# 64-column tiles and three early weight conversions in a gated linear attention with two MLPs

## The chip, the cores and the metric

The kernel runs on one core of a Trainium2 chip. The metric is the device time of one execution in microseconds. Five engines take part: PE (matmuls, with its weight loads shown apart as PEld), DVE (VectorE), ACT (ScalarE), POOL (GpSimd) and SP, which issues most DMAs. Each takes its own instructions in program order and waits on semaphores for the others.

## The reference

A linear attention with a decay for each key channel runs over 4 batches, 8 heads, 768 steps and 48 channels. Its output, laid out as 3072 tokens of 384, goes through two gated MLPs of 1536 hidden channels, the second after an RMS norm. The MLP weights come in double precision.

```python
def _attn_ref(q, k, v, alpha):
    for t in range(S):
        state = alpha[:, :, t, :, None] * state + np.einsum('bhd,bhe->bhde', k[:, :, t], v[:, :, t])
        y[:, :, t] = np.einsum('bhd,bhde->bhe', q[:, :, t], state)

def _moe_ref(x, w_gate, w_val, w_out):
    g = x @ w_gate
    silu = g * (1.0 / (1.0 + np.exp(-g)))
    val = x @ w_val
    return (silu * val @ w_out).astype(np.float32)

def _moe2_ref(x, w_gate, w_val, w_out, rms_g):
    rms = np.sqrt(np.mean(x * x, axis=-1, keepdims=True) + 1e-06)
    xn = x / rms * rms_g
    ...  # then as _moe_ref
```

## The kernel before

**Attention.** The sequence is cut into 24 chunks of 128 steps (`n`), with the four head pairs `p` side by side and the two heads of a pair on partitions 0 to 63 and 64 to 127. Inside a chunk the terms between steps are built in levels `b` = 1, 2, 4, ... 64 (`LEVELS`): at level b the second half of each block of 2b steps attends to the first half. `products` and `merge` on DVE keep the decays and scale q and k for each level, `copy_qk` on ACT packs the operands of a level, `scores` (L301) makes the score tiles on PE, `masks` (L314, DVE) and `copies_32`, `copies_64` (ACT) bring them to SBUF as `P`, and `outputs` (L357) multiplies them with v into the tile `Y` in PSUM. The first six chunks use all seven levels; the others use five and do the terms inside blocks of four steps directly on DVE (`direct_ops`), bringing them to PE over DRAM (`ydd`, `yn`). `own_terms` puts these terms into `Y` by three transposes (L342) and, from chunk 4 on, adds the terms of the carried state (L346). `kv` (L371) multiplies k^T with v for the new state; `state` (DVE) adds it up.

**Tiles of the array.** Outputs and state terms are made in 12 blocks of 32 columns of weights (`blocks32`), a block for each third of a pair's 96 columns; k^T v in 16 tiles of 32 columns; scores in tiles of 64 rows by 32 columns. All of this is fp32, which PE does in two records per matmul: 12 blocks of a level are 24 records.

**MLP.** `mlp_points` goes through the blocks of chunks (`BLOCKS`: 2, 2, 4, 4, 4, 4, 4 chunks for the first MLP, six of 4 for the second) and, in each, through the 12 slices `f` of the hidden channels: gate matmuls (tile g), silu on ACT (L704), value matmuls (tile v, both L697), multiplication s = s*v on DVE (L707), and, one slice late, the output matmuls (`out_piece`, L738). g and v have one PSUM buffer each, so the gate of the next slice waits for silu and its value for the multiplication. The first two blocks (`PLAIN`) use fp32 weights and 256 columns; later ones use weights split into two fp32r parts.

**Conversion.** `conv(0)` turns the double-precision weights of slice f into fp32 in three steps: ACT takes the absolute value (L169); ACT takes the exponent byte (L175) and DVE clamps (L176); DVE puts the bits together (L185, L191) and the load of slice f + 3 is issued on POOL's queue. The first three loads are issued on SP's queue when the generator starts.

**Order.** Everything is emitted in one hand-written order. `lead` does chunks 0 and 1 together, before any MLP work. `slot(s)` emits step T of chunk n, with T = s - 12(n - 1), twelve slots for each chunk: merges at T = 1 to 6, scores at 6 and 9, transposes of k at 12, own terms and part of the outputs at 14, k^T v and the rest at 16. Slots below `START` come before the MLP; the others are spread over its points, three for each f, so that a block of four chunks takes along 48 slots. While the first block runs, each point also takes 1.1 conversion steps (`CONV1`), and a gate matmul whose slice isn't converted forces the missing steps ahead of it:

```python
while first and self.ready32 <= f:
    next(self.cv[0])
```

In `lead` one conversion is done: three single steps at T == 5, after the outputs of levels 3 and 4, and after `split_x`. SP's queue loads in this order: q and k of chunks 0 and 1, the mask, the operands of the direct terms, the identity, all 14 tiles of v for the levels (`vl`), q and k of chunk 2, then nine pieces of raw weights.

Of the kernel before, what the change touches and what calls it, by code (L numbers as in the profile page):

```python
# [24 lines left out]
NP = H // 2  # L25
# [19 lines left out]
START = NS + 2  # L45
# [11 lines left out]
class Kernel:  # L57
# [94 lines left out]
    def conv(self, layer):  # L152
# [10 lines left out]
        R = {f: self.raw(layer, f) for f in range(ahead)}  # L163
# [111 lines left out]
    def scores(self, n, ls):  # L275
# [3 lines left out]
        for l in ls:  # L279
# [4 lines left out]
            if (n, part) not in self.sct:  # L284
                pool, tag = (self.ps, f"o{part}") if n == 1 else (self.ps2, "sc")
                self.sct[n, part] = pool.tile([128, 4, NP, 32], F32, tag=tag, name="sb" if part else "sa")
# [16 lines left out]

    def masks(self, n, ls):
        for l in ls:
# [4 lines left out]
            if n == 1:  # L310
                self.P[n, l] = p = self.second["pt"][:, l - NX] if l >= NX else self.second["ptx"][:, l]
            else:
                self.P[n, l] = p = self.pt[:, l - NX] if l >= NX else self.ptx[l]
            self.nc.vector.tensor_tensor(  # L314
# [5 lines left out]
    def copies_32(self, n):  # L320
        p32 = self.P[n, NL - 2] = self.second["pt32"] if n == 1 else self.pt32
        sc = self.sc.pop((n, NL - 2))
        for o in range(0, 128, 32):
            g = slice(o % 64, o % 64 + 32)
            self.nc.scalar.activation(out=p32[o:o + 32, :, g], in_=sc[o:o + 32], func=AF.Copy)
# [5 lines left out]
    def blocks32(self):  # L331

        for cb in range(3 * NP):
            yield cb // 3, slice(32 * (cb % 3), 32 * (cb % 3) + 32), cb // 4, 32 * (cb % 4)

    def own_terms(self, n):
# [7 lines left out]
        if n >= B:  # L344
            for p, e, kt, o in self.blocks32():
                nc.tensor.matmul(out=Y[o:o + 32, kt], lhsT=self.Sd[:, p].rearrange("d h e -> d (h e)")[:, e],  # L346
                                 rhs=self.q(n)[:, 0, p], start=False, stop=False, skip_group_check=True)

    def outputs(self, n, ls):
        for l in ls:  # L350
            b = LEVELS[l]
            if b < CDS[n]:
                continue
            pt = self.P.pop((n, l))
            for p, e, kt, o in self.blocks32():
                ov = self.Yt[n][o:o + 32, kt].rearrange("e (j u i) -> e j u i", u=2, i=b)[:, :, 1]
                self.nc.tensor.matmul(out=ov, lhsT=self.vl(n, l)[:, p, e], rhs=pt[:, p],  # L357
                                      start=False, stop=False, skip_group_check=True)
# [3 lines left out]
    def kv(self, n):  # L362

        nc = self.nc
        kv = self.ps.tile([128, NP, D], F32, tag="v", name="kv") if n == 1 else self.ps2.tile(
            [128, NP, D], F32, tag="sc", name="kv")
# [159 lines left out]
    def transposes(self, n):  # L526
        kp = self.kp[n] = self.ps.tile([128, NP, 128], F32, tag="g", name="kp") if n == 1 else self.ps2.tile(
# [13 lines left out]
    def lead(self):  # L541
# [6 lines left out]
        direct = {}  # L548
        for T in range(1, NL):
            for n in two:  # L550
                self.scores(n, [T - 1])
# [13 lines left out]
            if T == 5:  # L565
                next(self.cv[0])
        for n in two:
            self.scores(n, [NL - 1])
# [17 lines left out]
        next(self.cv[0])  # L586
        for n in two:
            self.kv(n)
        for n in two:
# [6 lines left out]
        self.load_qk(3)  # L596

# [157 lines left out]
    def run(self):  # L755
# [59 lines left out]
        for i in range(NS, START):  # L815
            self.slot(i)
# [100 lines left out]
```

## Time and profile before

| | us |
|---|---|
| median of 3 runs | 1140.61 |
| lowest, highest | 1139.85, 1142.17 |
| the profiled execution | 1139.1 |
| its span, first to last instruction | 1137.3 |

The profile gives, for one execution, each engine's busy time, groups of instructions by source line, the chain of waits that ended last, and every instruction in order of time. Weight loads overlap matmuls and stand apart. A matmul's recorded duration is the time through the whole array, so for small tiles many overlap and the spacing of starts tells the rate. "issue" as the releaser of a wait means that the engine waited for nothing that the profile shows.

### The profile page before, as it was taken

The page shows a single profiled execution, that of the slowest core. Times are in us where ns is not written, and L with a number is a line of the kernel's source. Part 1 is how long each engine was busy: PE and PEld are TensorE (multiplying, and loading weights), DVE is VectorE, ACT ScalarE, POOL GpSimd, SP SyncE. Part 2 cuts the span into 40 slices and gives each one's busy share as a digit, 9 for nine tenths or more (in the row PEclk, how much of TensorE's full clock was granted, in tenths as well). Part 3 has the DMA queues.
Part 4 walks back from the last instruction along what each step waited for, and adds up shares of the span by engine and source line. Part 5 has one row for each costly group of instructions (what it writes and reads, how often), then busy time and mean ns, then how long its engine had stood idle before and what let it go on. Part 6 is the DMA issues. An engine that isn't in the chain of part 4 may idle for free.

```text
span 1137.3 us, 29157 instructions
## 1 busy us (share of the span) xinstructions
PE 1086.9 (96%) x12756; PEld 891.1 (78%) x12756; DVE 652.7 (57%) x1350; ACT 413.8 (36%) x737; POOL 39.5 (3%) x69
## 2 busy tenths in 40 slices
PE   3688898999999999999999999999999999999997
PEld 3567787788888888887888888888888888888886
DVE  6588798777676766766746877723322323233221
ACT  3556544433343343334334444422231222322212
POOL 0121000000000000000000000000000000000000
PEclk9899999999999999999999999999999999999999
DMA  9677344543443454345315343110000000100000
GB/s 335 196 224 223 100 134 137 150 135 105 135 142 104 113 156 134 105 128 148 104 58 192 114 143 122 42 56 1 29 28 1 29 29 1 56 1 1 29 1 28
DMA packets 55665, 112.72 MB, mean 99 GB/s; under 512 B 7185, under 2 KB 38929, under 8 KB 55537
## 3 DMA queue, kind: packets, MB, share of 16 engines
q1 hardware_dynamic: 51072, 93.15, 27.2%
q0 software_dynamic: 4464, 17.70, 4.7%
q8 instruction: 100, 1.64, 0.6%
q14 instruction: 29, 0.23, 0.1%
HBM read 97.85 MB, written 12.98 MB: 97 GB/s over the span
## 4 chain that ended last, share of the span: by engine, by line
PE 82%; DMA 1%; issue 1%; DVE 1%; ACT 0%; POOLq 0%; DVEq 0%; ACTq 0%
PE g L697 25%; PE v L697 24%; PE o L738 24%; PE y L357 3%; PE sb L301 2%; PE y L346 1%; PE sa L301 1%; PE kv L371 1%; PE y L342 1%; DMA yn<-ydd 1%; PE rb L636 0%; PE kp L530 0%; PE ss L617 0%; DMA ydd<-yd 0%; DMA out<-ev 0%
## 5 line engine op out<-in xcount | busy, mean ns | idle before, releaser
L707 DVE TENSOR_TENSOR s<-s,v 128x512 f32<-128x512 f32 (+1 forms) x156 | 100.8, 646 | 371.2 <-PE v L697 370.0
L697 PE MATMUL g<-xhi,w 128*128 128x512 f32 x792 | 270.7, 396 | 0.0
L697 PE MATMUL v<-xhi,w 128*128 128x512 f32 x792 | 269.7, 395 | 0.0
L738 PE MATMUL o<-hh,w 128*128 128x512 f32 x792 | 201.8, 390 | 0.0
L704 ACT ACTIVATE s<-g 128x512 f32<-128x512 f32 (+1 forms) x156 | 88.1, 565 | 289.4 <-PE g L697 286.7
L713 ACT ACTIVATE hh<-s 128x512 fp32r<-128x512 f32 x132 | 83.5, 633 | 271.1 <-DVE s L707 271.0
L697 PEld LDWEIGHTS g<-xhi,w 128*128 128x128 f32 x792 | 148.6, 188 | 33.0
L697 PEld LDWEIGHTS v<-xhi,w 128*128 128x128 f32 x792 | 148.8, 188 | 32.4
L738 PEld LDWEIGHTS o<-hh,w 128*128 128x128 f32 x792 | 148.8, 188 | 31.7
L697 PE MATMUL v<-xlo,w 128*128 128x512 f32 x396 | 154.7, 391 | 0.0
L697 PE MATMUL g<-xlo,w 128*128 128x512 f32 x396 | 154.5, 390 | 0.0
L719 DVE TENSOR_TENSOR hl<-s,hh 128x512 fp32r<-128x512 f32 x132 | 91.0, 689 | 41.4 <-ACT hh L713 36.8
L738 PE MATMUL o<-hl,w 128*128 128x512 f32 x396 | 114.4, 397 | 0.2 <-DVE hl L719 0.2
L697 PEld LDWEIGHTS g<-xlo,w 128*128 128x128 f32 x396 | 74.5, 188 | 14.9
L697 PEld LDWEIGHTS v<-xlo,w 128*128 128x128 f32 x396 | 74.4, 188 | 14.7
L738 PEld LDWEIGHTS o<-hl,w 128*128 128x128 f32 x396 | 72.7, 188 | 16.6 <-DVE hl L719 0.6
L273 ACT ACTIVATE kc<-qk 128x512 f32<-128x512 f32 x69 | 43.7, 633 | 67.1 <-DVE qk L248 64.9
L248 DVE TENSOR_TENSOR qk<-qk,bpb 128x512 f32<-128x512 f32 x96 | 65.6, 683 | 4.3 <-ACT kc L273 2.2
L697 PE MATMUL g<-x,x 128*128 128x256 f32 x144 | 38.3, 403 | 16.2 <-DVE x L191 16.1
L357 PE MATMUL y<-pt,vl 128*32 128x64 f32 x2760 | 49.6, 222 | 2.3 <-issue 2.3
L357 PEld LDWEIGHTS y<-pt,vl 128*32 128x32 f32 x2760 | 44.0, 112 | 5.0 <-issue 4.3
L697 PEld LDWEIGHTS g<-x,x 128*128 128x128 f32 x144 | 26.8, 197 | 22.3 <-issue 16.9
(129 smaller groups left out, 1098.5 us busy)
## 6 DMA issues: line engine op xcount, KB each, us to landing
vl<-vl SPq DMA_DIRECT2D x115, 192.0 KB, 4.8
qk<-qka SPq DMA_DIRECT2D x42, 288.0 KB, 5.0
room<-w SPq DMA_DIRECT2D x27, 384.0 KB, 4.5
room<-w POOLq DMA_DIRECT2D x27, 384.0 KB, 4.3
dir<-dirx SPq DMA_DIRECT2D x54, 192.0 KB, 3.2
wraw<-w SPq DMA_DIRECT2D x18, 384.0 KB, 3.8
x2in<-x2d SPq DMA_DIRECT2D x6, 768.0 KB, 4.3
out<-ev SPq DMA_DIRECT2D x18, 256.0 KB, 2.0
```

The source lines that it names most:

```text
L248: self.nc.vector.tensor_tensor(out=v, in0=v, in1=sub(t, o, [(1, 2), (2, nb), (0, b)]), op=ALU.mult)
L273: self.nc.scalar.activation(out=sub(t, 0, [(NP * 64, 2), (b, NP * 64 // b), (1, b)]), in_=v, func=AF.Copy)
L301: nc.tensor.matmul(out=sc[o:o + 32, p], lhsT=kc[d, p, gs], rhs=qc[d, p, gs if b < 64 else slice(0, 64)], start=True, stop=True, skip_group ...
L342: nc.tensor.matmul(out=Y[:, k], lhsT=yn[:, 128 * k:128 * k + 128], rhs=self.ident, is_transpose=True, start=(k == 0), stop=False, skip_gro ...
L346: nc.tensor.matmul(out=Y[o:o + 32, kt], lhsT=self.Sd[:, p].rearrange("d h e -> d (h e)")[:, e], rhs=self.q(n)[:, 0, p], start=False, stop= ...
L357: self.nc.tensor.matmul(out=ov, lhsT=self.vl(n, l)[:, p, e], rhs=pt[:, p], start=False, stop=False, skip_group_check=True)
L697: nc.tensor.matmul(out=ps[:, :N], lhsT=a, rhs=x, start=(q == 0), stop=(q == len(ops) - 1))
L704: nc.scalar.activation(out=s[:, :N], in_=g[:, :N], func=AF.Silu)
L707: nc.vector.tensor_tensor(out=s[:, :N], in0=s[:, :N], in1=v[:, :N], op=ALU.mult)
L713: nc.scalar.activation(out=hh[:, :N], in_=s[:, :N], func=AF.Copy)
L719: nc.vector.tensor_tensor(out=hl[:, :N], in0=s[:, :N], in1=hh[:, :N], op=ALU.subtract)
L738: nc.tensor.matmul(out=O[gj][i][:, :N], lhsT=a[:, 128 * i:128 * i + 128], rhs=x[:, :N], start=(f == 0 and q == 0), stop=(f == NF - 1 and q ...
```

## The change

- `outputs`, the state terms in `own_terms` and `kv` use tiles of 64 columns where a head's columns allow: `columns(64)` gives four blocks of 64 columns, `columns(32)` the four of 32 that are left. In each call all blocks of 64 come first, then all of 32. `kv` uses 8 tiles of 64 columns.
- In chunks 0 and 1 `scores_two` makes 64 by 64 score tiles in place of pairs of 64 by 32, with whole masks; two levels share a PSUM tile, and the tiles lie in other PSUM buffers.
- The lead takes nine conversion steps instead of three, so slices 0, 1 and 2 stand ahead of the MLP in program order. One more slot (T = 2 of chunk 2) lies ahead of it too (`START`), each of the three slots behind a conversion step.
- The raw weights of the first slices are loaded earlier in SP's queue: slice 0 after eight of the 14 `vl` tiles, slice 1 after the other six, slice 2 after q and k of chunk 2.

```diff
-START = NS + 2
+START = NS + 3
...
-        R = {f: self.raw(layer, f) for f in range(ahead)}
+        R = {f: self.raw(layer, f) for f in range(ahead)} if layer else self.R0
...
+    def scores_two(self, l):
+        b = LEVELS[l]
+        for n in range(2):
+            if l % 2 == 0:
+                self.sct[n] = (self.ps2.tile([128, 2, NP, 64], F32, tag="sc", name="st") if l in (0, NL - 1) else
+                               self.ps.tile([128, 2, NP, 64], F32, tag=("g", "v", "o0", "o1")[l - 2 + n], name="st"))
+            t = self.sc[n, l] = self.sct[n][:, l % 2]
...
+            for p in range(NP):
+                for h in range(2):
+                    d = slice(64 * h, 64 * h + 64)
+                    self.nc.tensor.matmul(out=t[d, p], lhsT=k[d, p], rhs=q[d, p], start=True, stop=True,
+                                          skip_group_check=True)
...
-    def blocks32(self):
-
-        for cb in range(3 * NP):
-            yield cb // 3, slice(32 * (cb % 3), 32 * (cb % 3) + 32), cb // 4, 32 * (cb % 4)
+    def columns(self, w):
+        for p in (0, 2, 1, 3):
+            for e in ((0, 64) if p % 2 == 0 else (32, 0)):
+                if (w == 64) == (e == 32 or e == 0 and p % 2 == 0):
+                    o = 96 * p + e
+                    yield p, slice(e, e + w), o // 128, slice(o % 128, o % 128 + w)
...
     def outputs(self, n, ls):
+        ls = [l for l in ls if LEVELS[l] >= CDS[n]]
+        for w in (64, 32):
+            for l in ls:
+                for p, e, kt, o in self.columns(w):
+                    ov = self.Yt[n][o, kt].rearrange("e (j u i) -> e j u i", u=2, i=LEVELS[l])[:, :, 1]
+                    self.nc.tensor.matmul(out=ov, lhsT=self.vl(n, l)[:, p, e], rhs=self.P[n, l][:, p],
+                                          start=False, stop=False, skip_group_check=True)
...
-                for o in (64 * h, 64 * h + 32):
-                    nc.tensor.matmul(out=kv[o:o + 32, p], lhsT=kt[:, p, o:o + 32], rhs=vn[:, p, h],
-                                     start=True, stop=True, skip_group_check=True)
+                o = slice(64 * h, 64 * h + 64)
+                nc.tensor.matmul(out=kv[o, p], lhsT=kt[:, p, o], rhs=vn[:, p, h],
+                                 start=True, stop=True, skip_group_check=True)
...
         for n in two:
             self.outputs(n, range(3, 5))
-        next(self.cv[0])
+        step()
         for n in two:
             self.merge(n, LEVELS[-1])
             self.products(n, LEVELS[-1])
             self.transposes(n)
+        step()
...
-        next(self.cv[0])
         for n in two:
             self.kv(n)
+        step()
+        step()
         for n in two:
             self.state(n)
...
         self.load_qk(3)
+        step()
+        for i in range(NS, START):
+            step()
+            self.slot(i)
...
         for n in range(2):
-            for l in range(NL):
+            for l in range(4):
                 self.load_vl(n, l)
+        self.R0 = {0: self.raw(0, 0)}
+        for n in range(2):
+            for l in range(4, NL):
+                self.load_vl(n, l)
+        self.R0[1] = self.raw(0, 1)
         self.load_qk(2)
+        self.R0[2] = self.raw(0, 2)
```

## Rows read from the trace of the kernel before

**Rows 1.** The page: busy time of PE (part 1), the chain that ended last (part 4).
```profile
PE 1086.9 (96%) x12756; PEld 891.1 (78%) x12756; DVE 652.7 (57%) x1350; ACT 413.8 (36%) x737; POOL 39.5 (3%) x69
...
PE 82%; DMA 1%; issue 1%; DVE 1%; ACT 0%; POOLq 0%; DVEq 0%; ACTq 0%
```
**Rows 2.** Stretches: length, busy us (instructions) by engine, granted clock, DMA share, GB/s.
```profile
0.00:41.70 41.70, 20.36 (x862) 17.08 (x862) 23.12 (x53) 16.52 (x30) 2.49 (x9) 1.00 0.84 293
...
51.00:123.40 72.40, 62.38 (x1189) 51.76 (x1190) 58.76 (x97) 41.28 (x60) 13.57 (x24) 0.96 0.64 204
123.40:207.00 83.60, 77.43 (x1750) 64.00 (x1749) 70.39 (x160) 39.83 (x80) 2.60 (x4) 0.98 0.50 137
307.00:357.00 50.00, 50.00 (x850) 40.35 (x850) 35.23 (x87) 19.95 (x41) 2.60 (x4) 1.00 0.46 134
```
**Rows 3.** PE in time: start, us, line, tiles, weights, shape, count; chunk 9's attention.
```profile
245.27 0.49 PE L342 MATMUL y<-ident,yn 128*128 128x128 f32 x3
245.69 0.86 PE L346 MATMUL y<-qk,Sd 128*32 128x128 f32 x24
246.36 0.85 PE L357 MATMUL y<-pt,vl 128*32 128x64 f32 x48
247.15 0.50 PE L697 MATMUL g<-xhi,w 128*128 128x512 f32 x1
247.48 0.40 PE L697 MATMUL g<-xlo,w 128*128 128x512 f32 x1
...
249.43 0.55 PE L371 MATMUL kv<-vn,kt 128*32 128x48 f32 x32
249.80 1.19 PE L357 MATMUL y<-pt,vl 128*32 128x64 f32 x72
```
**Rows 4.** PE in time, the lead and the first MLP block; idle time before in brackets.
```profile
20.48 0.66 PE L301 MATMUL sb<-kc 64*32 64x32 f32 x32
...
28.98 0.34 PE L301 MATMUL sb<-qk 64*32 64x32 f32 x9 [3.10 <-issue]
...
34.36 0.77 PE L357 MATMUL y<-pt,vl 128*32 128x64 f32 x41 [1.37 <-issue]
...
41.52 0.28 PE L371 MATMUL kv<-more 128*32 128x48 f32 x3 [1.95 <-issue]
41.72 1.56 PE L697 MATMUL g<-x,x 128*128 128x256 f32 x6
43.12 1.46 PE L697 MATMUL v<-x,x 128*128 128x256 f32 x6
50.98 2.90 PE L697 MATMUL g<-x,x 128*128 128x256 f32 x6 [6.40 <-DVE x L191]
...
123.36 1.46 PE L697 MATMUL g<-x,x 128*128 128x256 f32 x6
```
**Rows 5.** The page, part 3: the queue that brings instructions.
```profile
q8 instruction: 100, 1.64, 0.6%
```
**Rows 6.** DVE in time, the first MLP block.
```profile
46.15 0.76 DVE L176 TENSOR_SCALAR x<-x 128x1152 f32<-128x1152 f32 x1 [0.32 <-ACT x L169]
46.82 0.41 DVE L707 TENSOR_TENSOR s<-s,v 128x256 f32<-128x256 f32 x1
...
48.09 1.36 DVE L185 SCALAR_TENSOR_TENSOR x<-x,room 128x1152 int32<-128x1152 int32 x1
49.48 1.36 DVE L191 SCALAR_TENSOR_TENSOR x<-room,x 128x1152 int32<-128x1152 int32 x1
...
55.41 0.42 DVE L707 TENSOR_TENSOR s<-s,v 128x256 f32<-128x256 f32 x1 [1.37 <-PE v L697]
...
104.29 0.42 DVE L707 TENSOR_TENSOR s<-s,v 128x256 f32<-128x256 f32 x1
```
**Rows 7.** The page, part 5: the group whose waits for conversions are added up.
```profile
L697 PE MATMUL g<-x,x 128*128 128x256 f32 x144 | 38.3, 403 | 16.2 <-DVE x L191 16.1
```
**Rows 8.** PE in time, the second MLP block: two of its waits.
```profile
176.55 0.62 PE L342 MATMUL y<-ident,yn 128*128 128x128 f32 x3 [2.40 <-DMA yn<-ydd]
...
206.53 0.38 PE L301 MATMUL sa<-kc 64*32 64x32 f32 x21 [1.30 <-issue]
```

More of the change, by code (lines that the diff above doesn't have):

```diff
@@ L284, in scores @@
             if (n, part) not in self.sct:
-                pool, tag = (self.ps, f"o{part}") if n == 1 else (self.ps2, "sc")
-                self.sct[n, part] = pool.tile([128, 4, NP, 32], F32, tag=tag, name="sb" if part else "sa")
+                self.sct[n, part] = self.ps2.tile([128, 4, NP, 32], F32, tag="sc", name="sb" if part else "sa")
             t = self.sct[n, part]
@@ L313, in masks @@
                 self.P[n, l] = p = self.pt[:, l - NX] if l >= NX else self.ptx[l]
+            if n < 2:
+                self.nc.vector.tensor_tensor(out=p, in0=self.sc.pop((n, l)),
+                                             in1=self.mask[:, l:l + 1].to_broadcast([128, NP, 64]), op=ALU.mult)
+                continue
             self.nc.vector.tensor_tensor(
@@ L324, in copies_32 @@
             g = slice(o % 64, o % 64 + 32)
-            self.nc.scalar.activation(out=p32[o:o + 32, :, g], in_=sc[o:o + 32], func=AF.Copy)
+            self.nc.scalar.activation(out=p32[o:o + 32, :, g], in_=sc[o:o + 32, :, g] if n < 2 else sc[o:o + 32], func=AF.Copy)
     def copies_64(self, n):
@@ L344, in own_terms @@
         if n >= B:
-            for p, e, kt, o in self.blocks32():
-                nc.tensor.matmul(out=Y[o:o + 32, kt], lhsT=self.Sd[:, p].rearrange("d h e -> d (h e)")[:, e],
-                                 rhs=self.q(n)[:, 0, p], start=False, stop=False, skip_group_check=True)
+            for w in (64, 32):
+                for p, e, kt, o in self.columns(w):
+                    nc.tensor.matmul(out=Y[o, kt], lhsT=self.Sd[:, p].rearrange("d h e -> d (h e)")[:, e],
+                                     rhs=self.q(n)[:, 0, p], start=False, stop=False, skip_group_check=True)
     def outputs(self, n, ls):
-        for l in ls:
[L351 to L358, printed above, removed]
+        ls = [l for l in ls if LEVELS[l] >= CDS[n]]
+        for w in (64, 32):
+            for l in ls:
+                for p, e, kt, o in self.columns(w):
+                    ov = self.Yt[n][o, kt].rearrange("e (j u i) -> e j u i", u=2, i=LEVELS[l])[:, :, 1]
+                    self.nc.tensor.matmul(out=ov, lhsT=self.vl(n, l)[:, p, e], rhs=self.P[n, l][:, p],
+                                          start=False, stop=False, skip_group_check=True)
+        for l in ls:
+            del self.P[n, l]
         if n == CDS.index(4) - 1 and NL - 1 in ls:
@@ L364, in kv @@
         nc = self.nc
-        kv = self.ps.tile([128, NP, D], F32, tag="v", name="kv") if n == 1 else self.ps2.tile(
+        kv = self.ps.tile([128, NP, D], F32, tag=f"o{n}", name="kv") if n < 2 else self.ps2.tile(
             [128, NP, D], F32, tag="sc", name="kv")
@@ L526, in transposes @@
     def transposes(self, n):
-        kp = self.kp[n] = self.ps.tile([128, NP, 128], F32, tag="g", name="kp") if n == 1 else self.ps2.tile(
+        kp = self.kp[n] = self.ps.tile([128, NP, 128], F32, tag="gv"[n], name="kp") if n < 2 else self.ps2.tile(
             [128, NP, 128], F32, tag="sc", name="kp")
@@ L547, in lead @@
             self.products(n, 1)
-        direct = {}
+        step = lambda: next(self.cv[0])
         for T in range(1, NL):
-            for n in two:
-                self.scores(n, [T - 1])
+            self.scores_two(T - 1)
             for n in two:
@@ L565, in lead @@
             if T == 5:
-                next(self.cv[0])
-        for n in two:
-            self.scores(n, [NL - 1])
+                step()
+        self.scores_two(NL - 1)
         for n in two:
@@ L596, in lead @@
         self.load_qk(3)
+        step()
+        for i in range(NS, START):
+            step()
+            self.slot(i)
     def norm_steps(self, j):
@@ L814, in run @@
         self.lead()
-        for i in range(NS, START):
-            self.slot(i)
         cur = None
```

5 lines of the change are left out of this document (4 added, 1 removed).

## The prediction

> **What bounds the kernel now.** I read the page first: TensorE (PE) is busy for nearly the whole span, and the chain that ended last runs over it for 82% [rows 1]. Busy time alone doesn't say what a stretch waits for, so the second view is the table of stretches [rows 2]. It shows three regimes. In the lead (0 to 41.7 us) PE works half the time. From 51.0 to 123.4, the first MLP block, PE is idle for 10.0 us while VectorE (DVE) works 58.8 of 72.4. From about 207 on PE is full: 50.00 of 50.00 in the sample stretch, with DVE at 35. So every PE nanosecond counts after 207, DVE's order counts before 123, and between them both are near full.
>
> The third view is PE in order of time through one chunk's attention in the full regime [rows 3]. The three transposes of L342 start at 245.27 and end 0.49 later; one of 128 columns takes 0.107 (half of the 0.214 below), so the third starts at 245.48. The first state pass (L346, 32 columns of weights) starts at 245.69, not at 245.59: **a drain of about 0.10 us where the tile shape changes** from 128 to 32 columns. From L346 to L357, both 128 by 32, there is none: 24 passes fill 0.67 us, and 24 x 0.107 / 4 is 0.64, so four passes run side by side and the rest, 0.03, is the first weight load. L357 confirms it: 72 passes in 1.19 us, of which a single one takes 0.22, are 13.7 ns each. A pass over 256 columns costs (1.46 - 0.39) / 5 = 0.214 [rows 4], 64 columns 0.0535, and that is 3.9 times 13.7 ns. Going back to 128 columns costs another 0.10 beyond the drain, because the first g takes 0.33 to the second start where the next take 0.23.
>
> The fourth view is PE in the lead [rows 4]. There are three stalls that nothing releases ("issue"): 3.10, 1.37 and 1.95 us. The instruction queue moved 1.64 MB in 100 transfers [rows 5]; over the 25512 PE records that is 64 bytes each, 256 instructions a transfer. The stalls fall where small tiles use instructions up fast while the DMA carries 293 GB/s [rows 2]: I read them as PE waiting for its own code.
>
> The last view is DVE in the first block [rows 6]: conversion, s multiply and slot work go through one queue in program order. PE waits there for L191, the conversion's end, nine times and 16.1 us in all [rows 7].
>
> **The change, part by part. 1. Tiles of 64 columns.** A level has 12 blocks of 32 now, 24 passes, four at a time: 6 steps of 0.056 us (four of the 13.7 ns above). After it are 4 blocks of 64 (8 passes, two at a time: 4 steps) and 4 of 32 (8 passes, four at a time: 2 steps). Again 6 steps. State terms come out as 6 steps of 0.109 both ways. k^T v goes from 32 passes in 8 steps to 16 passes in 8 steps, if the 64-column weight load (half of 0.107 = 0.054) keeps up with a 48-column step (0.043): 0 to 0.10 dearer, I take 0.05. **The work streams for as long as before; a third of the instructions go, but in the full regime no stall of PE for them is visible** (PE 50.00 of 50.00 [rows 2]), so that is worth nothing there.
>
> What is added are changes of tile shape. At T = 14 the order becomes 128, 64 and 32 (state), 64 and 32 (outputs), 128: three more changes. At T = 16: 128, 64 (k^T v, outputs), 32, 128: one more. No row shows 64 to 32. The nearest rows are the change to 32 columns, 0.10 and 0.03 for the load, so 0.12 to 0.13, and the change back to 128, 0.21. I take 0.12 into 32 and 0.15 into 64 (its load is twice as long); the ends are nothing (a 64-column tile as two neighbours of 32) and 0.21. Per chunk: T = 14 gives 2 x 0.12 + 0.15 + 0.03 (the first load is longer) = 0.42; T = 16 gives 0.12 + 0.03 + 0.05 = 0.20. Behind 207 us lie chunks 8 to 23, the last four without k^T v: 12 x 0.62 + 4 x 0.57 = 9.7. Chunks 6 and 7 add 1.2. Chunks 4 and 5 add nothing: PE waits 2.40 at 176.55 for yn to come over DRAM [rows 8], which absorbs them. Chunks 2 and 3 lie in DVE's stretch. **Sum +10.9, with ends of +2 and +17.**
>
> The Trainium skill, "TensorEngine Tiling (Array Packing)", Key Properties, says that changing the tiling mode, not just the tile, drains the engine. By that rule 64 to 32 drains as 128 to 32 does in the rows, the sum stands, and the zero end falls; it speaks against this change.
>
> **2. The lead.** Its PE instructions fall from 1724 (862 records of each kind [rows 2]) to 988: 224 passes of scores, 224 of outputs, 32 of k^T v and 14 transposes, each with a load. I let the three stalls go, -6.4. Against that, 64 by 64 score tiles run two at a time, where four 64 by 32 ran: the passes here take twice their later time ((0.66 - 0.24) / 31 = 13.5 ns a pass), which is the lower of the two clock levels, 1.2 of 2.4 GHz, though the column of the granted clock has 1.00 for this stretch; so a level of both chunks goes from 0.9 to 1.7, twice on the path: +1.6. With changes of shape, +0.2. The MLP's first matmul moves from 41.72 to about 37.
>
> There the gain stops. Behind it DVE has, in program order, the rest of f = 1 (L185 and L191, 1.36 each), all of f = 2 (0.76 + 1.36 + 1.36 [rows 6]), the states and slots 12 to 15: some 11 us from about 38.5, when ScalarE (ACT) has delivered its part. The first s multiply and the g of f = 1 stand behind that, as ACT's silu stands behind the copies of the same slots. s lands near 50 (46.82 now), g of f = 1 near 49.6 (50.98 now), the second s near 55.5 (55.41 now). POOL's loads of the weights for f = 3 and on follow each conversion and come earlier; SP's order of loads puts the first weights ahead of six vl tiles, which are wanted only at about 30 us. Both I cost at nothing; without that cover, one weight load of 1.18 MB at 293 GB/s is 4 us.
>
> **3. Conversions two ahead.** The rate stays 1.1 steps a point, so DVE's order per f is as now until f = 8 instead of 10. From the second to the ninth s takes 48.9 us (55.41 to 104.29); of the DVE idle in it, about 3.4 us come from PE being late, the rest from ACT. So the ninth lands at 55.5 + 45.5 = 101. After that no conversion is left and PE sets the pace: the 19.1 us to the next block's g at 123.36 [rows 4] shrink by the 2.4 that PE waits for L191 in them, to 16.7. The second block begins at 117.7: **-5.7**, with ends of -1 (DVE keeps its idle time) and -13 (PE sets the pace throughout). DVE's idle time at the end of the first block is what remains.
>
> **4. Later fetch stalls.** 1.30 at 206.53 [rows 8] and 0.24 before it lie in scores that stay as they are, but fewer instructions precede them: 0 to -1.5, I take -0.8.
>
> Sum on the profiled execution: 1139.1 + 10.9 - 5.7 - 0.8 = 1143.5, +4.4. That execution lies 1.5 below the median of 1140.6, so the median to expect is **1145.0**.
>
> **The rivals.** (a) *64 to 32 drains nothing*, since both are made of 32-column strips. Part 1 falls to +2, the sum is -4.5: 1136. For it: within one shape neighbouring strips run freely. Against: the drain from 128 to 32 is there although both use all 128 rows. (b) *PE sets the pace in the first block*: with conversions ahead, the 10.0 us of PE idle from 51.0 to 123.4 and the stretch at the lower clock (0.96 granted) go, and block two begins near 111, -12.5: 10.9 - 12.5 - 0.8 = -2.4, 1138. It decides where DVE's work per f (6.1) is below PE's (5.3 of matmuls and attention); the rows say above. (c) *Weight loads of the halves don't run side by side*: then 20 steps of outputs per chunk take 0.107 instead of 0.056 and k^T v 0.5 more, 1.5 us per chunk, 18 chunks, +27: 1172. Against: four 32-column loads already fit a 0.056 step, though 0.027 each. (d) *The lead's stalls stay*, because they are no matter of PE's code or because the DMA queues hold the next block back as before: part 2 loses its 6.4, DVE's chain begins some 3 us later, and the time is 1148. Against: 256 instructions of mostly 64-column work last twice as long. The Trainium skill, "Runtime: NRT & Kernel Launch", Instruction fetch mechanics, calls the cost of crossing a 16 KiB instruction block mostly hidden, which would make the stalls something else; the 3.10 and 1.95 us at such blocks do not agree with it. (e) *It doesn't do what it says*: f = 2 is converted only in program order when the MLP begins; that is in the forecast, which has DVE finish it some 10 us into the MLP.
>
> **How the numbers follow.** Forecast (1141 to 1151): 0.55. (a) 0.17, (b) 0.13, (c) 0.07, (d) 0.05, anything else 0.03. About 0.2%, 2.3 us, is what a measurement can tell from no change, so "same" is 1138.3 to 1142.9. Slower: 0.43 of the forecast, (c) and (d), together 0.55. Same: 0.11 of the forecast, 0.06 of (a), 0.06 of (b), 0.01: 0.24. Faster: 0.01, 0.11, 0.07, 0.02: 0.21. The range leaves out (c) and the far part of (a): 1135 to 1153.
>
> **What would show it.** PE in order of time past 207: one chunk's attention longer by 0.6 us, with about 0.1 between the 64- and the 32-column outputs; without that gap (a) is right. The lead: no issue stall over 1 us, the first g near 37, then a hole to about 50; if block two begins before 114, (b) has it. Steps of outputs at 0.107 mean (c). I'd be wrong altogether if attention past 207 got shorter: then instructions, not columns, set its pace.

## The result, and the profile after

| | before | after |
|---|---|---|
| median, runs side by side, us | 1141.39 (4 runs) | 1151.89 (4 runs) |
| lowest, highest | 1139.85, 1143.09 | 1149.75, 1152.57 |
| the profiled execution | 1139.1 | 1152.57 |
| its span | 1137.3 | 1150.8 |

The ratio is 1.0088, with a 95% interval of 1.0068 to 1.0109: slower, by 10.5 us in the medians. The two profiled spans lie 13.5 us apart: the profiled execution of before (1139.1) is shorter than all four of these runs, and that of after is the longest of its four. So some 3 us of the account below belong to these two executions. The forecast of 1145.0 had the sign and was 6.9 us short; as a difference it had 4.4 for 10.5. The median lies above the 1141 to 1151 that the forecast's own case covered, and inside the range of 1135 to 1153. For tiles64_only below, the median is that of three of its four runs: the fourth took 1379.08 us at a granted clock of 0.753.

The page of the kernel after: busy time of PE (part 1) and the queue that brings instructions (part 3).

```profile
PE 1105.8 (96%) x10996; PEld 899.0 (78%) x10996; DVE 653.0 (57%) x1350; ACT 412.8 (36%) x737; POOL 39.2 (3%) x69
...
q8 instruction: 86, 1.41, 0.5%
```

PE has 1760 records fewer than in [rows 1] and is busy 18.9 us longer. That is the first reading of this case: PE's busy time follows neither the instructions nor, as it turns out, the streamed columns alone.

The table of stretches after, cut where [rows 2] is cut: length, busy us (instructions) of PE, PEld, DVE, ACT, POOL, granted clock, DMA share, GB/s. The last line is the whole first block, from the first gate matmul of the MLP to that of block two.

```profile
0.00:37.10 37.10, 23.28 (x494) 20.09 (x494) 22.75 (x52) 16.75 (x31) 2.50 (x9) 0.86 0.89 317
49.90:121.80 71.90, 64.49 (x1045) 52.78 (x1046) 56.81 (x97) 37.81 (x58) 10.00 (x18) 0.93 0.57 186
307.00:357.00 50.00, 50.00 (x716) 39.66 (x716) 35.09 (x86) 19.61 (x41) 2.61 (x4) 1.00 0.45 124
...
37.15:121.79 84.64, 67.34 (x1060) 54.97 (x1057) 67.68 (x113) 45.34 (x67) 13.34 (x24) 0.90 0.63 199
```

The lead is 4.6 us shorter. The first block is 84.64 us long where it was 81.64 (41.72 to 123.36 in [rows 4]). In the full regime 716 records fill the 50 us that 850 filled.

PE in order of time after, the lead and the first block (start, us, line, tiles, weights, shape, count; idle time before in brackets):

```profile
31.85 0.35 PE L378 MATMUL y<-pt,vl 128*32 128x64 f32 x9 [1.26 <-issue]
...
37.15 1.56 PE L724 MATMUL g<-x,x 128*128 128x256 f32 x6
38.55 1.46 PE L724 MATMUL v<-x,x 128*128 128x256 f32 x6
49.92 2.93 PE L724 MATMUL g<-x,x 128*128 128x256 f32 x6 [9.91 <-ACT s L731]
52.65 1.59 PE L724 MATMUL v<-x,x 128*128 128x256 f32 x6
57.07 1.56 PE L724 MATMUL g<-x,x 128*128 128x256 f32 x6
...
71.81 2.93 PE L724 MATMUL g<-x,x 128*128 128x256 f32 x6 [4.68 <-ACT s L731]
```

Of the lead's stalls 1.26 is left. Then come the two holes of the first block, 9.91 and 4.68 us, both ended by silu. Each is followed by gate matmuls of 2.93 where the others take 1.5: the lower of the two clock levels, 1.2 GHz. In [rows 4] there is one such gate (50.98) in the rows shown.

PE in order of time after, chunk 9's attention, to be held against [rows 3] (L364 transposes, L369 state terms, L378 outputs, L394 k^T v; the view merges the 64- and the 32-column passes of a line into one row):

```profile
247.13 0.49 PE L364 MATMUL y<-ident,yn 128*128 128x128 f32 x3
247.55 1.01 PE L369 MATMUL y<-qk,Sd 128*64 128x128 f32 x16
248.49 1.04 PE L378 MATMUL y<-pt,vl 128*64 128x64 f32 x32
249.47 0.50 PE L724 MATMUL g<-xhi,w 128*128 128x512 f32 x1
...
251.73 0.67 PE L394 MATMUL kv<-vn,kt 128*64 128x48 f32 x16
252.23 0.48 PE L378 MATMUL y<-pt,vl 128*64 128x64 f32 x10
```

From the start of the transposes to the next gate matmul it is 2.34 us (247.13 to 249.47); before it was 1.88 (245.27 to 247.15). State terms take 0.94 from start to start where they took 0.67, outputs 0.98 where they took 0.79. k^T v takes 0.50 where it took 0.37. The step at T = 16 lasts 1.79 where it lasted 1.48, so the two steps of a chunk grew by 0.46 + 0.31; the period of a chunk past 272 us is 25.66 where it was 24.92, which makes it 0.74. The account below takes 0.76 a chunk.

PE's waits after 121.8 us, in total, times and longest:

```profile
PE y L364 <- DMA yn<-ydd: 4.3, 2, 2.3
PE o L765 <- ACT ev L685: 3.1, 3, 1.1
```

Before, the same two waits had 2.6 and 1.1 us behind 123.4, and 2.3 us of issue stalls that are gone now. **The account of the two spans**, each term beside its forecast; the line ahead of the sum is what the others leave over:

| term | forecast | profile |
|---|---|---|
| start of the first gate matmul | -4.6 | -4.57 |
| length of the first block | -1.1 | +3.0 |
| tiles, chunks 6 to 23 | +10.9 | +13.2 = 14 x 0.76 + 4 x 0.64 |
| later issue stalls | -0.8 | -2.3 |
| PE's waits for yn | 0 | +1.7 |
| PE's waits for evacuations (ev) | 0 | +2.0 |
| chunks 2 to 5 and the rest | 0 | +0.5 |
| sum | +4.4 | +13.5 |

### The profile page after: what moved, and what is told of

Same layout as the page of the kernel before. It is cut to its first block, busy times and chain, and to the rows that moved or that the text cites. A ratio compares the mean times of both kernels' runs of the same rounds, so it can differ in the third digit from the quotient of the medians.

```text
span 1150.8 us, 25628 instructions
## 1 busy us (share of the span) xinstructions
PE 1105.8 (96%) x10996; PEld 899.0 (78%) x10996; DVE 653.0 (57%) x1350; ACT 412.8 (36%) x737; POOL 39.2 (3%) x69
## 4 chain that ended last, share of the span: by engine, by line
PE 82%; DMA 2%; DVE 1%; issue 1%; ACT 0%; ACTq 0%; POOLq 0%; DVEq 0%
PE g L724 24%; PE v L724 24%; PE o L765 24%; PE y L378 3%; PE sb L300 2%; PE y L369 1%; PE sa L300 1%; DMA x2d<-ev 1%; PE kv L394 1%; PE y L364 1%; DMA yn<-ydd 1%; DMA ydd<-yd 1%; PE rb L663 0%; PE kp L553 0%; PE ss L644 0%
## 5 line engine op out<-in xcount | busy, mean ns | idle before, releaser
L724 PEld LDWEIGHTS g<-xhi,w 128*128 128x128 f32 x792 | 148.7, 188 | 33.1
L378 PE MATMUL y<-pt,vl 128*64 128x64 f32 (+1 forms) x1840 | 56.7, 226 | 1.3 <-issue 1.3
L378 PEld LDWEIGHTS y<-pt,vl 128*64 128x64 f32 (+1 forms) x1840 | 46.5, 125 | 9.9 <-issue 6.8
## 6 DMA issues: line engine op xcount, KB each, us to landing
vl<-vl SPq DMA_DIRECT2D x115, 192.0 KB, 4.1
dir<-dirx SPq DMA_DIRECT2D x54, 192.0 KB, 3.3
```

The lines of the kernel that those rows point to most:

```text
L724: nc.tensor.matmul(out=ps[:, :N], lhsT=a, rhs=x, start=(q == 0), stop=(q == len(ops) - 1))
```

## The experiments

The kernels ran on three occasions, each beside its own runs of the kernel before; so ratios to it are compared, and 0.001 is 1.1 us. The first four take the tiles apart, the next four the first block, the last four the lead and a better order.

**late32: the 64-column tiles undone behind the lead.**

```diff
-    def columns(self, w):
+    def columns(self, w, n):
+        if n > 1:
+            if w == 32:
+                yield from self.blocks32()
+            return
...
-                o = slice(64 * h, 64 * h + 64)
+                for o in ([slice(64 * h, 64 * h + 64)] if n < 2 else
+                          [slice(64 * h, 64 * h + 32), slice(64 * h + 32, 64 * h + 64)]):
```

> The changed kernel with 32-column tiles for state terms, outputs and k^T v in chunks 2 to 23; the lead, the loads and the nine early conversion steps stay as changed. Theory (the loss is all in the tiles of the full regime): a chunk's period past 272 us falls from 25.66 back to 24.92 us, and what the lead and the conversions gained stays (1.7 to 2.1 us at chunks 4 to 6), so about 1139, ratio to the kernel before 0.998. Rival (a part of the loss is a shift of order: PE's wait of 2.26 us for yn at chunk 7 and waits of some 2 us for ScalarE's evacuations come from the earlier start and not from the tiles): these waits stay, 1142 to 1144, ratio 1.000 to 1.002.

Measured: 1135.99 us, ratio 0.9967 (0.9955 to 0.9980), period 24.94. Beside the change's 1.0088 the tiles cost 0.0121, 13.8 us. The wait for yn at chunk 7 falls from 2.26 to 0.38 (that at chunk 6 stays, 2.21), and of the waits for evacuations one of 0.80 is left behind 200 us. Issue stalls of 2.3 us stand behind the first block again, where the changed kernel has none: the wider tiles had taken these away. The theory holds, and the shift of order by itself carries no loss; lead and conversions keep 3.7 us of gain, more than the 1.7 to 2.1 expected.

**tiles64_only: the other half, the kernel before with the tiles from chunk 2 on.**

```diff
-            for p, e, kt, o in self.blocks32():
+            for w in (64, 32):
+                for p, e, kt, o in self.columns(w, n):
...
+                for o in ([slice(64 * h, 64 * h + 64)] if n > 1 else
+                          [slice(64 * h, 64 * h + 32), slice(64 * h + 32, 64 * h + 64)]):
```

`columns(w, n)` gives the 12 blocks of 32 for chunks 0 and 1.

> The kernel before with 64-column tiles for state terms, outputs and k^T v in chunks 2 to 23 alone; lead, loads and conversions as before. Theory (tiles carry the loss, 0.74 us a chunk over 16 chunks past 207 us and up to 1 us in chunks 6 and 7, and the waits for evacuations come with them): 1141.4 + 13 to 15.5, so 1154 to 1157, ratio 1.012 to 1.014, slower than the full change by what lead and conversions give. Rival (the shift of order carries the waits): 1141.4 + 11.8, ratio 1.010 at most, and PE's wait for yn at chunk 7 is as short as before (0.20).

Measured: 1151.88 us, ratio 1.0109 (1.0093 to 1.0125), between the two. PE waits 2.34 for yn at chunk 7, so that wait comes with the tiles; the wait for ev at 219.7 doesn't appear. From both sides the tiles are worth 12.4 to 13.8 us.

**grouped: two changes of shape fewer at T = 14.**

```diff
+        for w in (64, 32):
+            if n >= B and 3 in ls:
+                self.state_terms(w)
             for l in ls:
                 for p, e, kt, o in self.columns(w):
```

> The changed kernel with the order 64 (state terms, then outputs), 32 (state terms, then outputs) at T = 14: the same matmuls with two changes of tile shape fewer in each of chunks 4 to 23. Theory (each change of shape drains PE): the 2.34 us from the first transpose to the next gate matmul fall by 0.12 + 0.15 = 0.27 to 2.07; over 16 to 18 chunks 4.3 to 4.9 us, so about 1147. Rival (the 64-column passes themselves are slower than two at a time, changes cost next to nothing): 2.3 us stay, 1152.

Measured: 1145.99 us, ratio 1.0046 (1.0032 to 1.0060), 4.8 us less than the change. PE in order of time, chunk 9 (L368 state terms, L380 outputs), where this order lets the shapes be seen apart:

```profile
245.96 0.49 PE L364 MATMUL y<-ident,yn 128*128 128x128 f32 x3
246.38 0.66 PE L368 MATMUL y<-qk,Sd 128*64 128x128 f32 x8
246.86 0.63 PE L380 MATMUL y<-pt,vl 128*64 128x64 f32 x16
247.43 0.43 PE L368 MATMUL y<-qk,Sd 128*32 128x128 f32 x8
247.67 0.41 PE L380 MATMUL y<-pt,vl 128*32 128x64 f32 x16
248.01 0.50 PE L726 MATMUL g<-xhi,w 128*128 128x512 f32 x1
```

2.05 us in place of 2.34. Within one shape there is no gap: the 64-column state terms hand over after 0.48, which is 4 steps of 0.109 and a first load. Then the 16 outputs of 64 columns, 8 steps of two that start 0.058 apart, 0.47 in all, take 0.57 until the first pass of 32 columns starts, and the two steps of state terms behind it take 0.24 where 2 x 0.109 is 0.22. That is 0.10 of drain and 0.02 for a longer first step: **0.12 for the change from 64 to 32**, as the forecast had it. The other change that went, from 32 back to 64, has 0.29 - 0.12 = 0.17 left, where the forecast took 0.15. Rival (a), that 64 to 32 drains nothing, falls. The rule of the Trainium skill, "TensorEngine Tiling (Array Packing)", Key Properties, that a change of the tiling mode drains the engine, agrees with these 0.12.

**kv32: k^T v back to 32 columns, with the same number of changes of shape.**

```diff
-        for w in (64, 32):
+        for w in ((32, 64) if n > 1 and 4 in ls and n + B < NCH else (64, 32)):
```

> The changed kernel with k^T v in 32-column tiles for chunks 2 to 19, followed by the 32-column outputs and then the 64-column ones, so that T = 16 keeps the number of changes of shape. Theory (the 64-column k^T v is held back by its weight loads, 0.501 us in place of 0.365): each of these chunks gets 0.14 back, less up to 0.03 for the longer first load behind the last change, 12 to 14 chunks, so 1.3 to 1.9 us less, about 1150. Rival (the 0.136 is the price of the change into 64 columns and stays with the outputs): 1152.

Measured: 1145.84 us, ratio 1.0056 (1.0043 to 1.0068). PE in order of time, chunk 9:

```profile
248.10 0.55 PE L395 MATMUL kv<-vn,kt 128*32 128x48 f32 x32
248.46 1.37 PE L378 MATMUL y<-pt,vl 128*32 128x64 f32 x48
249.76 0.50 PE L725 MATMUL v<-xhi,w 128*128 128x512 f32 x1
```

k^T v takes 0.36 again, and T = 16 lasts 1.66 where it lasted 1.79: 0.13 a chunk, as expected. The time fell by 3.6 us, more than that explains: in this kernel PE waits 0.66 for yn at chunk 7 where it waited 2.26, and not at 219.7 for ev.

**one_conversion: late32 with the conversions at the places of the kernel before.**

```diff
-START = NS + 3
+START = NS + 2
...
             self.transposes(n)
-        step()
...
+        step()
         for n in two:
             self.kv(n)
-        step()
-        step()
...
-        step()
         for i in range(NS, START):
-            step()
             self.slot(i)
```

> The kernel of late32 (32-column tiles from chunk 2 on, the changed lead) with one conversion in the lead, at the places of the kernel before, and two slots ahead of the MLP. Theory (two conversions more ahead of the MLP are worth little, because VectorE's waits for TensorE turn into waits for ScalarE): 0 to 1.5 us longer than late32, the second block begins between 121 and 124 us. Rival (they are worth the 5.7 us forecast, and something else in the changed lead eats it): 4 to 6 us longer than late32, the second block begins near 126.

Measured: 1133.06 us, ratio 0.9951 (0.9937 to 0.9965), 1.8 us *shorter* than late32. Both expectations missed: being two conversions and one slot ahead costs time. The edit takes the slot back with the conversions, so the two aren't told apart; no_slots below, which takes back two slots more, is no faster. The first s multiply is at 42.07 (48.39 in late32), and block two begins at 117.98 (119.41), though its lead ended 1.7 us later. The block itself is 81.03 us long, in late32 84.14.

**silu_first: silu of the first block issued ahead of the slot and the conversion step.**

```diff
-                yield gj, f, 0
+                early = gj == (0, 0)
+                if not early:
+                    yield gj, f, 0
...
                 nc.scalar.activation(out=s[:, :N], in_=g[:, :N], func=AF.Silu)
+                if early:
+                    yield gj, f, 0
```

> The kernel of late32 with ScalarE's silu of the first block issued right behind its gate matmuls, ahead of the slot and the conversion step that follow the gate. Theory (silu waits in ScalarE's order behind copies that wait for VectorE): TensorE's waits for silu in the first block, 15.1 us in the changed kernel, fall to some 8 to 10; the wait of 4.7 at 71.8 goes, the first one (9.9) stays for the most part since VectorE's s multiply of f = 0 ends it; the second block begins 2 to 4 us earlier. Rival (VectorE's own order sets the pace, whatever ScalarE's is): the waits change their name to s, and the second block begins within 1 us of late32.

Measured: 1136.33 us, ratio 0.9975 (0.9963 to 0.9987), no better than late32. PE's wait of 4.4 us for silu at the fourth slice becomes one of 5.60 for s (DVE L747) at 72.64, and block two begins at 120.71, 1.3 us later than in late32 where the rival had it within 1 us. The waits change their name, as the rival said, and nothing is gained.

**no_dve_conv: VectorE's part of nine conversions left out.**

```diff
+            bare = layer == 0 and f > 2
+            if not bare:
+                nc.vector.tensor_scalar(out=xf, in0=xf, scalar1=W_MIN, scalar2=W_MAX, op0=ALU.max, op1=ALU.min)
```

The two operations at L185 and L191 stand behind the same condition, and ScalarE's first pass has another scale for these slices.

> The kernel of late32 with VectorE's three operations of a conversion left out from slice 3 on (ScalarE's two passes and the loads stay); the weights of these slices are not the reference's, so the output isn't either. Theory (VectorE and ScalarE in their written order set the pace of the first block): 9 conversions x 3.5 us go from VectorE, TensorE sets the pace from the second gate on, and the second block begins 8 to 11 us earlier than in late32, near 111. Rival (TensorE's work and the lower clock set it already): less than 3 us.

Measured: 1126.66 us, ratio 0.9894 (0.9877 to 0.9911), 8.3 us less than late32. Block two begins at 112.78, 6.6 us earlier; the lead happened to end 1.6 us later than in late32, and from the first gate it is 8.2 (75.92 for 84.14), at the lower end of the 8 to 11 expected. Behind the hole of 9.89, which stays, PE's waits in the block are 0.51 for silu and 1.25 of issue. VectorE's conversions do set the pace, as the theory has it.

**act_first: late32 with ScalarE's passes of a conversion one step earlier.**

```diff
-            nc.scalar.activation(out=xf, in_=hi.bitcast(F32), func=AF.Abs, scale=65536.0)
+            if layer or f < 4:
+                nc.scalar.activation(out=xf, in_=hi.bitcast(F32), func=AF.Abs, scale=65536.0)
+            else:
+                exponent(f)
...
+            if layer == 0 and 3 <= f < NF - 1:
+                xn = self.xtile(layer, f + 1)
+                nc.scalar.activation(out=xn, in_=R[f + 1][:, :, 1].bitcast(F32), func=AF.Abs, scale=65536.0)
```

`exponent` is the pass of L175; the second part stands behind L191.

> The kernel of late32 with ScalarE's two passes of a conversion issued one step earlier from slice 4 on (the absolute value of slice f + 1 in the last step of slice f, the exponent in the first step of its own slice); VectorE's order stays. Theory (between the second and the ninth s VectorE stands 5.7 us idle for these two passes, 4.6 and 1.1): these waits go, the ninth s lands near 101 in place of 105, the second block begins 3 to 5 us earlier than in late32. Rival (the idle time moves on to ScalarE's copies or to TensorE): within 1 us of late32.

Measured: 1131.36 us, ratio 0.9943 (0.9927 to 0.9959), 2.7 us less than late32. The ninth s lands at 100.64 (late32: 103.37), and block two begins at 116.68, 2.7 us earlier where 3 to 5 were expected. The lead ended 1.3 us later here than in late32: from the first gate it is 80.13 us, 4.0 less than late32's 84.14. The stretch from the second to the ninth s, 44.2 us for 47.8, carries 3.6 of it. The theory holds.

**one_act_first: the two findings together, one conversion and ScalarE a step earlier.**

```diff
-            if layer or f < 4:
+            if layer or f < 2:
...
-            if layer == 0 and 3 <= f < NF - 1:
+            if layer == 0 and 1 <= f < NF - 1:
```

The diff is against act_first; the lead is that of one_conversion.

> The kernel of one_conversion (32-column tiles from chunk 2 on, the changed lead, one conversion ahead) with ScalarE's two passes of a conversion issued a step earlier, here from slice 2 on. Theory (VectorE's idle time for ScalarE, 4.3 and 1.1 us in that kernel's first block, is the term that the order can give back, with one conversion ahead as with three): the second block begins 2 to 4 us earlier, at 114 to 116, and the time falls by as much, to about 0.993 of the kernel before. Rival (with one conversion ahead TensorE waits for L191 and VectorE's idle time lies where TensorE is late): within 1 us of one_conversion.

Measured: 1128.72 us, ratio 0.9910 (0.9896 to 0.9925). Block two begins at 115.13, 2.9 us earlier than in one_conversion, as expected. The ratio is lower by 0.0041, 4.7 us; the 1.8 us beyond block two stay open. This version beats both kernels: it keeps the change's lead, drops the 64-column tiles behind it and the early conversions. The first block in the table of stretches, here and in one_conversion and act_first:

```profile
36.76:115.13 78.37, 64.06 (x1203) 53.03 (x1201) 66.47 (x112) 46.11 (x67) 13.85 (x25) 0.96 0.69 215
```
```profile
36.95:117.98 81.03, 63.91 (x1204) 52.91 (x1201) 66.46 (x111) 46.12 (x67) 13.55 (x24) 0.96 0.65 207
```
```profile
36.55:116.68 80.13, 65.62 (x1205) 54.15 (x1202) 67.27 (x113) 45.60 (x67) 14.11 (x25) 0.91 0.67 210
```

DVE has 66.5 to 67.3 us of work in each of them, and 67.68 in the changed kernel. What differs is its idle time: 11.9, 14.6 and 12.9 us, and 17.0 in the changed kernel.

**loads_only: the kernel before with the raw weights loaded earlier.**

```diff
-            for l in range(NL):
+            for l in range(4):
                 self.load_vl(n, l)
+        self.R0 = {0: self.raw(0, 0)}
+        for n in range(2):
+            for l in range(4, NL):
+                self.load_vl(n, l)
+        self.R0[1] = self.raw(0, 1)
         self.load_qk(2)
+        self.R0[2] = self.raw(0, 2)
```

> The kernel before with the raw weights of slices 0 to 2 loaded at the places of the changed kernel, nothing else. Theory (TensorE's stalls in the lead are waits for its own code, and fewer instructions took them away): the issue stalls of the kernel before (3.10, 1.37 and 1.95 us) stay, 5 us or more in all, the first gate matmul starts between 40.5 and 43 us. Rival (the order of the loads took them away): less than 2.5 us of stalls, the first gate matmul before 39.

Measured: 1139.11 us, ratio 0.9998 (0.9988 to 1.0007). The stalls are 3.68, 0.82 and 1.39, the first gate is at 40.84. The order of the loads does nothing that shows in the time.

**tiles_lead_only: one_conversion with the loads of the kernel before.**

```diff
-        R = {f: self.raw(layer, f) for f in range(ahead)} if layer else self.R0
+        R = {f: self.raw(layer, f) for f in range(ahead)}
...
-        self.R0 = {0: self.raw(0, 0)}
...
-        self.R0[1] = self.raw(0, 1)
         self.load_qk(2)
-        self.R0[2] = self.raw(0, 2)
```

> The kernel of one_conversion with the raw weights loaded at the places of the kernel before, so that the lead has the 64-column tiles alone. Theory (fewer instructions took the stalls away): at most 2 us of issue stalls in the lead, the first gate matmul within 1.5 us of that kernel's 36.95. Rival (the order of the loads has its share): it starts at 39 or later.

Measured: 1132.12 us, ratio 0.9935 (0.9921 to 0.9949). No issue stall of 0.4 us or more is left in the lead, and the first gate is at 36.04. With loads_only this settles it: the new tiles of the lead, with a little over half the instructions, took the stalls away.

**no_slots: one_act_first with nothing of chunk 2 ahead of the MLP.**

```diff
-START = NS + 2
+START = NS
```

> The kernel of one_act_first with no slot of chunk 2 ahead of the MLP (START = NS, where the kernel before has two and the changed kernel three). Theory (work that stands on VectorE ahead of the first s multiply costs TensorE, which can't get the time back): 2.8 us of VectorE go behind the first s, TensorE's wait before the second gate falls by 2 to 3 us, the second block begins 1 to 3 us earlier. Rival (only the sum of VectorE's work up to the last conversion counts): the second block begins within 0.7 us of one_act_first.

Measured: 1131.79 us, ratio 0.9931 (0.9919 to 0.9944), no faster than one_act_first and by the medians 3.1 us slower. PE's wait before the second gate falls from 6.42 to 4.14, as the theory said, and block two begins at 115.37 against 115.13, as the rival said: the wait is paid later, 2.73 in place of 1.50 before the third gate. The lead ended earlier here (first gate at 35.40 against 36.76), so the block itself is 1.6 us longer.

## Why the forecast fell short

**Part 1, tiles: right in kind, 2.3 us too small.** The drains were priced right: T = 14 grew by 0.46 where 0.42 was forecast, and grouped took two changes away for 0.29. The term that was mis-sized is k^T v. I took 0.05 for it, between 0 and 0.10; it took 0.13 (0.50 against 0.37, and kv32 gave 0.13 back). PE in order of time after, chunk 9, the 14 passes of k^T v behind the first two:

```profile
251.82 0.58 PE L394 MATMUL kv<-vn,kt 128*64 128x48 f32 x14
```

A single one takes 0.22, so the last starts 0.36 behind the first; by the single starts in the trace it is 0.058 from one pair to the next, where a step of four 32-column passes took 0.043. The 64-column outputs go at 0.058 a pair too, so streaming 48 columns is no cheaper there than streaming 64. That fits the cause that the forecast had named, a weight load that must keep up with the step, at 0.058 and not 0.054; no run shows the load by itself. Seven such steps are 0.11 dearer, and the rest of the 0.13 lies in the first step. So T = 16 grew by 0.31 and not 0.20, and a chunk by 0.76 and not 0.62: of the 0.14 that was missing, k^T v is 0.08 and T = 14 is 0.04. Rival (c), loads of the halves one behind the other at 0.107 a step, is out: the 64-column outputs in grouped go at 0.058.

**Part 2, the lead: right, but for its last number.** The first gate is at 37.15 where about 37 was said, one stall of 1.26 is left where the prediction's last paragraph had none over 1, s of f = 0 is at 50.31 (near 50), the gate of f = 1 at 49.92 (near 49.6). That the first gate agrees to 0.2 us is partly luck: late32 has the same lead and its first gate at 35.27. The second s is at 57.46 where near 55.5 was said:

```profile
50.31 0.41 DVE L734 TENSOR_TENSOR s<-s,v 128x256 f32<-128x256 f32 x1
...
57.46 0.41 DVE L734 TENSOR_TENSOR s<-s,v 128x256 f32<-128x256 f32 x1
...
105.27 0.42 DVE L734 TENSOR_TENSOR s<-s,v 128x256 f32<-128x256 f32 x1
```

Between the first two, DVE has 5.93 us of work and stands 1.2 idle for ACT. The forecast gave these 7.15 us only 5.5, less than DVE's own work there, which was 6.06 before the change.

For the stalls, loads_only and tiles_lead_only show that the reason was right too, and rival (d) falls: stalls of 5.9 us stand with the old instructions and the new loads, none with the new instructions and the old loads. The trace of the kernel before says the same of its three long stalls: its DMA view has one 16 KiB transfer of instructions in each of 26.4 to 27.6, 31.9 to 33.1 and 39.3 to 40.3 us, and the stalls end at 28.98, 34.36 and 41.52, each 1.2 to 1.5 us behind the end of one. Here the trace goes against the Trainium skill, "Runtime: NRT & Kernel Launch", Instruction fetch mechanics, which calls the crossing of an instruction block mostly hidden; with many small matmuls it was 5.9 us of a 41 us lead.

**Part 3, the conversions: the step that failed.** The forecast took 3.4 us of DVE's idle time, in which PE was late, out of the stretch from the second to the ninth s, and so put the ninth at 101 and block two at 117.7. PE was late no more, and those waits did go: PE waits no longer for L191 at all. But the ninth s came at 105.27. The stretch before and after, in the columns of [rows 2]:

```profile
55.41:104.29 48.88, 41.29 (x790) 33.88 (x789) 42.20 (x66) 25.85 (x37) 11.98 (x21) 0.97 0.71 232
```
```profile
57.46:105.27 47.81, 40.55 (x587) 32.84 (x586) 41.64 (x65) 26.43 (x40) 8.41 (x15) 0.93 0.61 205
```

DVE's idle time was 6.7 us (42.20 busy of 48.88) and is 6.2 (41.64 of 47.81); only the name at its end changed. So the stretch takes 47.81 where 45.5 was forecast, 2.3 us more. Of the 4.1 us by which block two is late (121.79 for 117.7), these are one half and the second s, 2.0 late, is the other; behind the ninth s the forecast held (16.5 us for 16.7). After, what ends most of it is ACT's passes, as the two queues show around 68 us. ACT in order of time after:

```profile
67.72 1.10 ACT L345 ACTIVATE pt<-sb 32x128 f32<-32x128 f32 x4 [6.90 <-DVE pt L334]
68.83 0.39 ACT L349 ACTIVATE pt<-sb 128x256 f32<-128x256 f32 x1
69.11 1.23 ACT L169 ACTIVATE x<-room 128x1152 f32<-128x1152 f32 x1
70.23 1.26 ACT L175 ACTIVATE room<-room 128x1152 int32<-128x1152 uint8 x1
71.37 0.39 ACT L731 ACTIVATE s<-g 128x256 f32<-128x256 f32 x1
```

And DVE in the same stretch:

```profile
67.27 0.42 DVE L334 TENSOR_TENSOR pt<-sb,mask 128x256 f32<-128x256 f32 x1
67.60 0.68 DVE L248 TENSOR_TENSOR qk<-qk,bpb 128x512 f32<-128x512 f32 x1
70.38 0.76 DVE L176 TENSOR_SCALAR x<-x 128x1152 f32<-128x1152 f32 x1 [2.09 <-ACT x L169]
```

ACT stands 6.90 us idle ahead of a copy that waits for DVE's masks; when the masks come, its copies go first, and DVE waits 2.09 for the absolute value that stands behind them; silu stands behind both passes, and PE's wait of 4.68 ends with it, at 71.81. Over the stretch DVE waits 4.6 us for L169 and 1.1 for L175. act_first shows that this was the cause: with these passes a step earlier the stretch takes 44.2 us where late32's takes 47.8 and the forecast had 45.5, and block two begins 80.1 us behind the first gate, where the forecast had 80.6 (117.7 - 37.1). A wait had taken the place of the one removed, and I had written "the rest from ACT" as if it were fixed.

Beside that, the forecast took for a gain what one_conversion shows to be a cost. Nine steps ahead of the MLP in program order are not ahead of it in time: DVE has 67.68 us of work between the first gate and block two, and 66.42 before the change. Two conversions only moved in front of the first s multiply. With them come the holes of 9.91 and 4.68 us (one_conversion has 6.43 as its longest), and behind the holes the clock is granted lower: 0.90 over the first block where it was 0.94, and in late32 0.88 where one_conversion has 0.96. The first block of late32, to be held against one_conversion's above:

```profile
35.27:119.41 84.14, 67.22 (x1205) 54.87 (x1201) 67.68 (x113) 45.50 (x67) 13.43 (x25) 0.88 0.64 200
```

PE's own work in the block is 67.22 us in late32 and 63.91 in one_conversion, at nearly the same idle time (16.9 and 17.1). That part of the cost, some 3 us, goes with the clock; no run changed the clock alone. no_slots speaks against a simple rule: its first hole is shorter than that of one_act_first (4.14 against 6.42), and yet its clock is 0.94 against 0.96. Rival (b), a second block that begins near 111, did not come: 121.79. Only no_dve_conv, without DVE's part of nine conversions, gets near it, with 112.78.

**Part 4: right, and larger.** The stalls of 1.30 and 0.24 went, 2.3 us in all where 0.8 was taken. late32, with the old tiles behind the lead, has 2.3 us again, and tiles64_only none.

**What stood in no term.** PE's waits for yn and for ev cost 3.7 us more than before. The forecast used yn only at 176.55 (chunk 6), where a wait hides the new drains of chunks 4 and 5. That a wait could become longer wasn't in the sum. The evacuation waits of 1.14 at 219.73 and 0.84 at 700.44 stay open; grouped has the first too (1.10), late32 one of 0.80 elsewhere, kv32 and tiles64_only neither at 219.7.

## What to carry to other kernels

In this kernel wider tiles saved instructions, and that was worth time only where PE stalled for its code; where PE is full, count the changes of tile shape per loop and put equal shapes side by side, at 0.12 to 0.17 us for each change here. Work moved ahead in program order is not ahead in time when its engine is already behind: compare the engine's busy time in the stretch before and after, and ask which idle time it is to fill. When one wait is taken out of a loop over two in-order engines, look in the other queue for what the freed engine will wait for next, and cost that too.

## What the runs showed of the hardware that was not expected

A transfer of instructions may hold up loads. The DMA view after, 190.9 to 192.0 us, with the one 16 KiB transfer, and then the issues of 188.6 to 190.9 (KB each, median us to landing):

```profile
q8 instruction: 1, 0.02, 5.5%
```
```profile
dir<-dirx SPq DMA_DIRECT2D x3, 192.0 KB, 4.6
ydd<-yd POOLq DMA_DIRECT2D x1, 192.0 KB, 5.2
```

The same issues in late32, 186.8 to 190.4 us; there the transfer comes after 190.4, when they have landed or nearly so:

```profile
dir<-dirx SPq DMA_DIRECT2D x3, 192.0 KB, 3.3
ydd<-yd POOLq DMA_DIRECT2D x1, 192.0 KB, 3.6
```

At chunk 7 the instruction transfer falls among these loads in the changed kernel, in tiles64_only and in grouped, 1.6 to 2.4 us behind the issue of ydd, and the load of yn is issued 5.7 to 5.9 us behind the issue of ydd; in the eleven others it falls 3.6 us or more behind, and yn follows after 4.0 to 4.3. Where it falls seems to go with the number of PE's instructions ahead of it. No run moved the transfer by itself, so this is read from the traces, not shown by a test.
